# Whole 128x128 transposes with one wide copy each, and GpSimd for the normalization, in a gated linear attention + spatial gating kernel

## The chip, the cores and the metric

The kernel runs on one core of a Trainium2 chip, in one launch. The metric is the device time in microseconds (us); lower is better. The time before is 144.26 us, the median of three runs (143.81 to 145.1).

## What is computed

Two layers follow each other. The first is a gated linear recurrence over 768 steps for 4 batches and 8 heads of width 48; its output is laid out as x (768 rows of 384 per batch). The second is a gated MLP whose second half is normalized per row and mixed along the sequence.

```python
for t in range(S):
    state = alpha[:, :, t, :, None] * state + np.einsum('bhd,bhe->bhde', k[:, :, t], v[:, :, t])
    y[:, :, t] = np.einsum('bhd,bhde->bhe', q[:, :, t], state)
...
h = np.maximum(x @ w_in, 0.0)
u, v = (h[..., :d_ff // 2].copy(), h[..., d_ff // 2:].copy())
v_n = (v - mu) / np.sqrt(var + 1e-06)
v_s = np.einsum('ts,bsd->btd', w_spatial, v_n) + b_spatial[None, :, None]
gated = u * v_s
return (gated @ w_out).astype(np.float32)
```

## The kernel before

**The recurrence in chunks.** Each batch has 6 chunks of 128 steps, 24 in all. Within a chunk the recurrence is done by matmuls: cumulative sums of log(alpha) (`cum`, TensorE), their exponentials (`einv`, `eexp`, ScalarE), the scaled k and q (`kt`, `qt`), the transposes of both (`tr`), scores k·q (`sc`), a causal mask on VectorE (`m`, `ms`), the product with v plus the part that comes from the old state (`y`), and a copy of the result as xT (`xe`). The state goes from chunk to chunk by `upd` (TensorE), `z` (VectorE, an add out of PSUM), `S` (multiply by the decay) and `sb` (a bf16 copy).

**Three layouts of chunks.** Chunks 0 and 1 are a *pair* (`pair`, j = 0): two chunks are loaded together, two steps to a partition, so that 64 partitions hold a chunk. Chunks 2 to 5 and 6 to 9 are two *groups of four* (`four_chunks`, j = 1 and 3), 32 partitions to a chunk. All others are loaded one by one (`single`, called from `two_singles`). In the pair and in the groups of four, k and q are turned by transposes of 64 rows: for each half of the partitions (`r`) one transpose per head pair, 16 for each of k and q and each half group, into two PSUM banks, and each bank is copied by its own instruction of 128x512 (`ev`, lines 564 to 568 and 780 to 789).

**The MLP.** Per batch and chunk: `v` (x times the second half of w_in, 3 matmuls of 512 columns), `ve` (relu into v_sb), `bn` (statistics, VectorE), `rs` (1/sqrt(var), two ScalarE steps for two chunks at a time), `vn` (subtract and multiply: the normalized rows, line 1103), and `u` for the other half, transposed. `s` mixes along the sequence with w_spT as the moving operand: part 0 takes the first four chunks of vn, part 1 the last two. `se` adds the bias, `g` multiplies with u, `o` is the product with w_out, `oe` its copy and `st` the store.

**What sets the order.** All operations are listed once with their dependencies, and the text `PLAN` is then read word by word: a letter for the engine (P TensorE, D VectorE, A ScalarE, G GpSimd, S the DMA queue), the operation's number, and for TensorE the PSUM banks. Every engine does its words in this order. Parts such as `:512#2` are matmuls on a tile `junk` (line 247) that feed nothing. Each w_* weight is loaded into one of two buffers `raw_w` (fetch, line 1052), cast to bf16 on some engine, and the buffer's next load waits for these casts: w_in (two halves), w_spatial (three pieces, turned into w_spT by `wt` and `we`), w_out.

Of the kernel before, what the change touches and what calls it, by code (L numbers as in the profile page):

```python
# [16 lines left out]
BF16 = mybir.dt.bfloat16  # L17
# [30 lines left out]
D154 S16 A143 A14 G13 D165 S274 P162@5,2 G155 D166 G17 G18 S20 A169 P54@3 A55 P96@0 A163 D157 A97 P183@2,1 A19
P170@4,3 S23 S276 D184 D185 D172 G158 D160 P99@5 A100 P167@2 A168 P177@0,6 P175@1,5 A182 A176 D171 D179 P188@2 P193@7
A189 A194 D178 D190 D101 D98 P197@1 A198 G159 G156 P173@6 A174 G161 P186@7 A187 P180@1 P199@6 A181 P222@1 D223 G278  # L50
A281 A200 D201 A102 P206@7 A207 D208 G279 P218@0 P209@1 G21 P34@7,6 A219 S389 S275 A202 D203 A210 G280 G10 G22 P191@0
P216@2 A282 D36 D35 A192 P37@1,6 A38 D211 A212 D103 D105 D104 D39 D213 G24 P40@7,4 A42 A217 P286@5 D41 D204 D205
P220@0 D221 P292@1 A287 D215 A293 G25 P43@3,6 D45 D44 D214 A294 D306 P283@7 P289@4 A284 A285 A288 A290 P236@2 P195@0
G305 G299 P232@6 P237 A291 G397 D297 P228@3 S26 P229 P233 D300 D303 G27 A28 A295 A196 D238 G296 G302 P317@4,5 P46@1,7
A318 P49@2,0 D230 D48 D234 G231 D47 G235 A319 A51 S387 S277 P224@3 S29 P225 D226 G227 A50 G301 P314@1,5 P311@0,6 D315
D312 P308@2,4 D310 A304 P248@3 P249 A309 D250 P340@4,2 D342 D341 A316 A30 P334@5,0 A313 D335 D336 P244@1 S493 P245
P240@6 S386 A390 A298 G32 S398 A31 G239 A497 P241 P391@5 A392 S388 S399 A393 A402 D242 D246 G307 P320@4,2,3,7 D321
G322 G395 D33 A394 D323 S400 S496 S505 S401 D324 G325 P332@6,0 A339 A333 P252@1 P253 P403@4 A404 D254 D326 D396 G406
A405 P262@2 A263 D407 P259@0 A260 P343@1 P337@3 A338 D344 P345@5,2 S495 S547 A346 S559 A352 P353@0,6 D354 D355 G327
G255 G328 G251 S550 S506 P409@4,3 A411 A410 D329 P347@5,1 D349 D348 P412@2 P358@0 P256@6 A257 P361@7 A359 P420@4,1  # L60
P415@5,6 G330 D331 D413 A509 P350@0 A351 P356@2 A357 D421 P498@4 S494 A362 A501 P368@0 P373@2 A369 P371@7 A551 D416
D422 G243 G247 D417 G408 G414 S549 P423@0 P418@6 D504 S507 A424 A499 A500 P510@1 A511 P265@0 D363 A372 S560 A513 A266
D419 D503 A512 P379@6 P441@5 A380 P425@7 A426 P428@0 P268@6 P435@7 D360 D370 S508 A364 S548 S622 S561 S613 A442 A429
D381 A382 D365 D366 D367 P377@4 P375@5 D515 S717 A436 A269 S623 S610 S611 S562 G514 G502 D427 D430 A376 A378 A431 D383
D384 P520@0 P437@1 A438 S625 P517@7,3 A563 D385 D432 P439@5 P552@4 P271@6 D519 D521 D433 A553 P447@1 P564@0 P451@3
D434 P448 P452 A554 A374 D557 A565 G568 A566 A272 S783 P455@2 P456 P443@6 G522 G621 A555 A518 P523@7,4 A440 S612 D556
D453 D569 A626 A567 P532@5,3 D457 D449 D525 D524 D533 D534 G516 S720 S624 P571@2,1 A573 A572 G454 G458 P444 P627@4
P528@0 D529 D445 S729 G558 A614 P467@7 P468 P526@5 A527 G450 G446 P535@3 D469 A536 A721 A628 G630 P578@0,2 D580 G470
D579 S771 S846 P587@1,6 P615@5 D530 A616 P574@7 P540@3 A541 P722@2 P537@0 A617 P475@3 D575 D588 A538 A570 S261 P463@7
A632 A618 S718 S719 G576 P583@1 D589 A531 D584 P481@0 P459@6 D620 G619 P636@5 P471@1 P472 A787 P464 P460 A482 A723  # L70
D539 D542 D473 A577 A629 A476 P581@0 P590@1 D631 S834 S732 S730 A725 P633@4,3 G585 A586 S731 D637 D465 G638 G466 A582
A733 P592@0 A591 P603@1 P734@7 D634 D728 D461 D462 A635 P644@6,3 P639@4,5 D645 A593 A737 A604 A543 A735 P599@0 A600
A724 D640 G474 G738 P487@1 P490@6 P597@0 A491 D641 P642@5 A736 D646 P647@3 A643 D594 D727 D544 D605 A488 A648 P484@6
A775 P649@1 D650 D651 D546 P652@3 S773 A653 A485 D654 D545 A606 D607 D608 D609 P595@2 A596 P663@1 P776@3 A779 S784
P665@6 A666 P478@5 P659@2 G726 G740 P601@6 D739 D602 A777 A660 P788@4 P679@2 P661@7 P744@6 A479 A778 D781 A655 S772
S785 D656 D664 D745 A789 A790 A791 G792 D658 D662 P667@5 P741@1,3 P675@6 D793 S835 A657 P676 P752@4 P668 D677 G780
# [24 lines left out]
SMALL = ()  # L101
# [1170 lines left out]
```

## Time and profile before

| | |
|---|---|
| median of three runs | 144.26 us (143.81 to 145.1) |
| the profiled execution | 145.11 us |
| its span in the trace | 142.5 us |
| TensorE busy | 133.9 us (94%) |
| VectorE busy | 121.6 us (85%) |
| ScalarE busy | 108.6 us (76%) |
| GpSimd busy | 83.6 us (59%) |
| `junk` matmuls (line 247) | 11.7 us in the page's groups |

The profile is of one execution. The span runs from the first to the last recorded instruction; the profiled execution lasted 2.6 us longer than its span. PE is TensorE, PEld its weight loads, DVE VectorE, ACT ScalarE, POOL GpSimd, SP the engine whose queue issues the DMAs. Matmuls are pipelined, so that a row's duration for a group includes about 0.17 us in which the next group already runs; the distance from one start to the next is the cost. L1010 is a helper (`accumulate`) for all of `v`, `u`, `s` and `o`, L192 one for all products, L181 and L183 for all copies of ScalarE and of the two others: such groups are told apart by their tiles.

### The profile page before, as it was taken

How to read it: one execution, taken by the hardware profiler on the slowest of the kernel's cores; microseconds unless marked ns; L12 is line 12 of the kernel's file. 1: busy time of each engine (PE TensorE's matmuls, PEld its weight loads, DVE VectorE, ACT ScalarE, POOL GpSimd, SP SyncE). 2: the span in 40 equal slices, each digit the busy share in tenths (PEclk: the TensorE clock that was granted, in tenths of full speed). 3: DMA queues.
4: the chain of work that ended last, by engine and by line, in shares of the span. 5: the costliest groups of instructions: out<-in, count | busy, mean ns of one | idle time of the engine just before them, and what ended most of it. 6: DMA issues, size and time to landing. Idle time of an engine off the chain costs nothing.

```text
span 142.5 us, 5286 instructions
## 1 busy us (share of the span) xinstructions
PE 133.9 (94%) x2124; PEld 80.9 (57%) x2136; DVE 121.6 (85%) x281; ACT 108.6 (76%) x253; POOL 83.6 (59%) x138
## 2 busy tenths in 40 slices
PE   7999979999989999799999998999999999999990
PEld 3546545565656656565667556656665765555560
DVE  6398697999997999989989999989979999877820
ACT  3465867999979889689998998879978666853261
POOL 7363695799489589813077956700599665000970
PEclk9999999999999999999999999999999999999999
DMA  4999992899999898989999998979930341027044
GB/s 114 335 365 362 391 391 66 265 373 294 301 238 291 165 207 170 192 167 178 201 211 205 187 208 161 229 211 247 187 60 5 110 162 66 5 94 292 0 164 167
DMA packets 76520, 28.64 MB, mean 201 GB/s; under 512 B 63057, under 2 KB 74961, under 8 KB 76497
## 3 DMA queue, kind: packets, MB, share of 16 engines
q1 hardware_dynamic: 76464, 28.32, 75.9%
q8 instruction: 16, 0.26, 0.7%
q14 instruction: 8, 0.06, 0.1%
q0 software_dynamic: 32, 0.00, 0.0%
HBM read 23.60 MB, written 4.72 MB: 199 GB/s over the span
## 4 chain that ended last, share of the span: by engine, by line
PE 67%; DVE 12%; DMA 8%; issue 4%; POOL 4%; ACT 3%; ACTq 0%; DVEq 0%; POOLq 0%; SPq 0%
PE bank L1010 44%; DMA raw_w<-in_moe_w_spatial_dram 8%; PE bank L247 5%; DVE qt L192 2%; PE bank L965 2%; PE bank L993 2%; DVE ptm L954 2%; POOL ac L192 2%; PE bank L948 2%; PE bank L438 1%; DVE zs L415 1%; PE bank L723 1%; PE bank L936 1%; PE bank L905 1%; PE bank L800 1%
## 5 line engine op out<-in xcount | busy, mean ns | idle before, releaser
L1010 PE MATMUL bank<-w_spT,vn 128*128 128x384 bf16 x192 | 35.3, 326 | 0.1
L192 POOL TENSOR_TENSOR kt<-kc,binv 128x384 bf16<-128x384 f32 x22 | 20.2, 932 | 25.9 <-ACT binv L912 19.0
L192 POOL TENSOR_TENSOR gT<-vs,uT 128x384 bf16<-128x384 f32 x28 | 26.6, 969 | 14.6 <-DVE vs L1159 14.6
L1010 PEld LDWEIGHTS <-vn 128*128 128x128 bf16 x192 | 17.7, 97 | 11.6 <-issue 0.6
L181 ACT COPY kqT<-bank 128x1024 bf16<-128x1024 bf16 (+1 forms) x23 | 17.9, 812 | 4.7 <-PE bank L777 1.9
L1159 DVE TENSOR_TENSOR vs<-bank,bsp_bc 128x384 f32<-128x384 f32 x31 | 16.4, 549 | 3.8 <-PE bank L1010 2.7
L1010 PE MATMUL bank<-xT,w_in 128*128 128x384 bf16 x96 | 19.4, 326 | 0.0
L1010 PE MATMUL bank<-w_out_sb,gT 128*128 128x384 bf16 (+1 forms) x100 | 18.4, 319 | 0.0
L954 DVE TENSOR_TENSOR ptm<-bank,mask 128x512 bf16<-128x512 f32 x28 | 17.6, 678 | 0.1
L1010 PE MATMUL bank<-w_in,xT 128*128 128x512 bf16 x60 | 16.7, 379 | 1.0 <-issue 0.2
L1072 DVE BATCH_NORM_STATS2 stats<-v_sb 128x6 f32<-128x512 bf16 x24 | 16.3, 680 | 0.6 <-ACT v_sb L187 0.5
L187 ACT ACTIVATE uT<-bank 128x384 bf16<-128x384 f32 x25 | 12.1, 489 | 4.8 <-PE bank L1010 4.8
L187 ACT ACTIVATE v_sb<-bank 128x512 bf16<-128x512 f32 x22 | 13.1, 602 | 1.7 <-PE bank L1010 1.4
L192 DVE TENSOR_TENSOR qt<-qc,bank 128x384 bf16<-128x384 f32 x24 | 12.4, 542 | 2.3 <-ACT bank L514 1.8
L181 ACT CAST xT<-bank 128x384 bf16<-128x384 f32 x20 | 9.2, 482 | 4.7 <-PE bank L438 3.9
L1010 PEld LDWEIGHTS <-gT 128*128 128x128 bf16 x100 | 9.3, 97 | 6.2
L247 PE MATMUL bank<-junk 128*128 128x512 f32 (+5 forms) x22 | 11.7, 653 | 1.0 <-DVE quarters_of L324 1.0
L1010 PEld LDWEIGHTS <-w_in 128*128 128x128 bf16 x96 | 8.8, 98 | 6.5
L850 DVE TENSOR_TENSOR ptm<-bank,mask 128x512 bf16<-128x512 f32 x16 | 10.1, 679 | 0.3 <-PE bank L842 0.2
L1010 PEld LDWEIGHTS <-xT 128*128 128x128 bf16 x72 | 6.4, 97 | 6.1 <-ACT xT L181 0.6
L415 DVE TENSOR_TENSOR zs<-bank,state 128x384 f32<-128x384 f32 x16 | 8.7, 545 | 0.1
L1103 DVE TENSOR_SCALAR vn<-v_sb,mvs,rstd 128x512 bf16<-128x512 bf16 x21 | 8.1, 419 | 0.2 <-ACT rstd L1083 0.2
(165 smaller groups left out, 260.6 us busy)
## 6 DMA issues: line engine op xcount, KB each, us to landing
vc<-in_v_dram SPq DMA_DIRECT2D x14, 192.0 KB, 3.9
kc<-in_k_dram SPq DMA_DIRECT2D x14, 192.0 KB, 4.2
ac<-in_alpha_dram SPq DMA_DIRECT2D x14, 192.0 KB, 4.3
qc<-in_q_dram SPq DMA_DIRECT2D x14, 192.0 KB, 4.6
raw_w<-in_moe_w_spatial_dram SPq DMA_DIRECT2D x3, 768.0 KB, 4.9
out_dram<-raw_w SPq DMA_DIRECT2D x11, 192.0 KB, 2.1
out_dram<-o_sb SPq DMA_DIRECT2D x9, 192.0 KB, 2.0
ac<-in_alpha_dram SPq DMA_DIRECT2D x2, 768.0 KB, 8.0
```

Of the source, the lines that this page charges most:

```text
L181: nc.scalar.copy(out=out, in_=in_)
L187: nc.scalar.activation(out=out, in_=in_, func=AF.Relu)
L192: ENG[eng].tensor_tensor(out=out, in0=in0, in1=in1, op=ALU.mult)
L247: nc.tensor.matmul(out=banks[n][:, 0:cols].rearrange("p (a b) -> p a b", a=4), lhsT=junk, rhs=junk[:, None, 0:cols // 4].to_broadcast([128 ...
L415: lambda _: nc.vector.tensor_tensor(out=zs[i % 3], in0=tp(), in1=state[(i - 1) % 3], op=ALU.add),
L850: nc.vector.tensor_tensor(out=ptm[n2][:, ci, s], in0=banks[sl.bank].rearrange("p (hp t) -> p hp t", hp=HP), in1=mask[:, 3][:, None, :].to_ ...
L948: nc.tensor.matmul(out=pt[s][:, hp, :], lhsT=kT[rows, hp, :], rhs=qT[rows, hp, :], start=True, stop=True)
L954: nc.vector.tensor_tensor(out=ptm[n2][:, ci, s], in0=banks[sl_p[s].bank].rearrange("p (hp t) -> p hp t", hp=HP), in1=mask[:, 2][:, None, : ...
L1010: nc.tensor.matmul(out=ps, lhsT=lhsT, rhs=rhs, start=first and n == 0, stop=last and n == len(pairs) - 1)
L1072: nc.vector.bn_stats(out=stats[tt % 2], in_=v_sb[n2][:, tt, :])
L1103: nc.vector.tensor_scalar(out=vn[n2][:, x, :], in0=v_sb[n2][:, x, :], scalar1=mvs[n2][:, x, 0:1], scalar2=rstd[n2][:, x:x + 1], op0=ALU.su ...
L1159: nc.vector.tensor_tensor(out=vs[d], in0=banks[sl.bank][:, 0:TH], in1=bsp_bc[:, th, :], op=ALU.add)
```

## The change

**Transposes.** In `pair` and `four_chunks` the 16 transposes of 64 rows become 8 of 128 rows by 128 columns, into one PSUM bank, and the two copies of 128x512 become one of 128x1024 (`evs`). Ten such sets are concerned (k and q of j = 0, and of the two halves of j = 1 and j = 3): 80 fewer transposes, 20 narrow copies less, 10 wide ones more. So that one copy can fill what were two tiles, `kqT[0]` and `kqT[1]` are now two views of one tile `kq`.

**Normalization.** `vn` may run on GpSimd, by the same instruction as on VectorE.

**The order table** is new throughout. VectorE did 21 of the 24 `vn` and does 5; ScalarE did 3 and does 1; GpSimd does 18. The `junk` columns go from 4512 to 3248. Some 70 other operations change engine, mostly in both directions; on balance GpSimd gets two more state copies and four more casts of v. PAIRS, QUADS and the dependencies of the other operations stand as they were. Lines below the first edit are up to five lower than before.

```diff
 PLAN = """
-D4 G9 D0 D3 G6 D2 S56 A60 G11 G5 P61@0:512#0:512#0:288#0 A63 A64 P62@1 A65 D1 D8 A67 A66 S58 D69 S57 S106 G71 D68
...
+D2 G6 G11 D0 S56 A60 G9 G5 P61@0:512#0:512#0:288#0 D4 D3 A63 D1 G7 D8 P62@1 A65 A66 P54@2:232#2 S57 D68 S58 D72 S59
...
-    kqT = sb("kqT", 2, [128, 2, 2, HP * 128])
+    kq = consts.tile([128, 2, 2, 2, HP * 128], BF16, name="kq")
+    kqT = [kq[:, :, 1 - x] for x in range(2)]
...
-            sls = [Slot(), Slot()]
-
-            def tr(_, src=(kt, qt)[n], sls=sls):
-                to = [half_words(sl, 8, 64) for sl in sls]
+            sl_w = Slot()
+
+            def tr(_, src=(kt, qt)[n], sl=sl_w):
+                to = half_words(sl, 16, 64).rearrange("p (r x) t -> p r x t", r=2)
                 for par in range(2):
                     for hp in range(HP):
-                        for r in range(2):
-                            rows = half(r)
...
-                                nc.tensor.transpose(
-                                    to[r][:, HP * par + hp, :], src[rows, par, hp].rearrange("p s d -> p (s d)"),
-                                    ident[rows, rows])
...
+                        nc.tensor.transpose(
+                            to[:, :, HP * par + hp, :], src[:, par, hp].rearrange("p s d -> p (s d)"), ident)
...
+            o = op(("evs", nm, j), "DVE ACT",
+                   lambda e, n=n, sl=sl_w: copy(
+                       e, kqT[n2][:, n].rearrange("p r x -> p (r x)"), banks[sl.bank].bitcast(BF16)),
+                   [("tr", nm, j)] + old_turned, use=[sl_w])
             for r in range(2):
-                op(("ev", nm, j, r), "DVE ACT",
-                   lambda e, n=n, r=r, sl=sls[r]: copy(e, kqT[n2][:, n, r], banks[sl.bank].bitcast(BF16)[:, 0:512]),
-                   [("tr", nm, j)] + old_turned, use=[sls[r]])
+                made[("ev", nm, j, r)] = o
...
+                def ev(e, n=n, x=x, sl=sl_w):
+                    to = kq[:, n].rearrange("p z ci (hp t) -> p (z ci) hp t", hp=HP)[:, :, :, 64 * x:64 * x + 64]
+                    copy(e, to, banks[sl.bank].bitcast(BF16).rearrange("p (zc hp t) -> p zc hp t", zc=4, hp=HP))
...
-                nc.vector.tensor_scalar(
+                ENG[e].tensor_scalar(
                     out=vn[n2][:, x, :], in0=v_sb[n2][:, x, :], scalar1=mvs[n2][:, x, 0:1],
                     scalar2=rstd[n2][:, x:x + 1], op0=ALU.subtract, op1=ALU.mult)
 
-            op(("vn", b, x), "DVE ACT", vnf,
+            op(("vn", b, x), "DVE ACT POOL", vnf,
```

**Where the order moves: VectorE in the pair.** The first rows are those of before, from the pair's first product with q; `ptm` are the masked scores, `state_128<-bank` is `S` of chunk 0, `zs` is `z` of chunk 1, and the last rows are the products with q of the first group of four.

```order
L192 TENSOR_TENSOR qt_106<-qc,bank_64 128x8x48
L192 TENSOR_TENSOR kt_104<-kc,binv_108 128x8x48
L192 TENSOR_TENSOR qt_106<-qc,bank_65 128x8x48
L183 COPY kqT_112<-bank_64 128x512
L183 COPY kqT_112<-bank_67 128x512
L183 COPY kqT_112<-bank_65 128x512
L602 TENSOR_TENSOR ptm_117<-bank_65,mask 128x512
L602 TENSOR_TENSOR ptm_117<-bank_64,mask 128x512
L602 TENSOR_TENSOR ptm_117<-bank_67,mask 128x512
L183 CAST bsp_bc<-bank_69 128x384
L602 TENSOR_TENSOR ptm_117<-bank_66,mask 128x512
L192 TENSOR_TENSOR state_128<-bank_66,bc_119 128x384
```

And the same place of the change:

```order
L191 TENSOR_TENSOR kt_104<-kc,binv_108 128x8x48
L191 TENSOR_TENSOR qt_106<-qc,bank_65 128x8x48
L191 TENSOR_TENSOR qt_106<-qc,bank_64 128x8x48
L182 COPY kq<-bank_67 128x1024
L191 TENSOR_TENSOR state_127<-bank_65,bc_118 128x384
L415 TENSOR_TENSOR zs_125<-bank_68,state_127 128x384
L595 TENSOR_TENSOR ptm_116<-bank_69,mask 128x512
L595 TENSOR_TENSOR ptm_116<-bank_67,mask 128x512
L595 TENSOR_TENSOR ptm_116<-bank_64,mask 128x512
L595 TENSOR_TENSOR ptm_116<-bank_66,mask 128x512
L191 TENSOR_TENSOR qt_106<-qc,bank_70 128x8x48
L191 TENSOR_TENSOR qt_106<-qc,bank_68 128x8x48
```

Three narrow copies have become one wide one, the state of chunk 0 and the sum for chunk 1 stand ahead of the masked scores instead of behind them, and the bias copy (`bsp_bc`) has gone to ScalarE.

**ScalarE ahead of the first w_in cast.** Before, from the last exponential of the first group of four to the casts that free the weight buffers:

```order
L749 ACTIVATE bank_67<-bank_67 128x384
L181 CAST xT_134<-bank_66 128x384
L181 COPY kqT_113<-bank_70 128x4x2x64
L181 CAST o_sb_158<-vc 128x384
L181 COPY kqT_112<-bank_65 128x4x2x64
L181 COPY kqT_112<-bank_69 128x4x2x64
L181 COPY kqT_113<-bank_68 128x4x2x64
L181 COPY kqT_112<-bank_64 128x4x2x64
L181 CAST w_in_88<-raw_w_96 128x512
```

Of the change:

```order
L744 ACTIVATE bank_64<-bank_64 128x384
L180 CAST bsp_bc<-bank_67 128x384
L180 COPY kq<-bank_71 128x16x64
L180 CAST o_sb_157<-vc 128x384
L180 COPY kq<-bank_68 128x16x64
L180 CAST xT_133<-bank_69 128x384
L180 CAST xT_133<-bank_66 128x384
L180 CAST w_in_88<-raw_w_96 128x512
```

Five narrow copies ahead of the cast have become two wide ones; a bias copy and a second xT copy have come in.

**GpSimd ahead of the first mix.** Before, from the last of the products of alpha for the second group of four; `w_row` are casts of w_spatial:

```order
L192 TENSOR_TENSOR ac<-ac 128x8x48
L355 MEMSET le_one 128x128
L356 AFFINE_SELECT le_one<-le_one 128x128
L355 MEMSET mask 128x128
L356 AFFINE_SELECT mask<-mask 128x128
L183 CAST w_row_94<-raw_w_96 128x768
L183 CAST w_row_95<-raw_w_97 128x768
L183 CAST w_row_93<-raw_w_97 128x768
L192 TENSOR_TENSOR kt_104<-kc,binv_109 128x8x48
L192 TENSOR_TENSOR kt_105<-kc,binv_111 128x8x48
L183 CAST vb_116<-vc 128x8x48
L183 CAST w_row_94<-raw_w_96 128x768
```

Of the change:

```order
L191 TENSOR_TENSOR ac<-ac 128x8x48
L182 CAST w_row_93<-raw_w_97 128x768
L182 CAST w_row_95<-raw_w_97 128x768
L1098 TENSOR_SCALAR vn_141<-v_sb_139,mvs_145,rstd_147 128x512 x4
L191 TENSOR_TENSOR kt_104<-kc,binv_109 128x8x48
L191 TENSOR_TENSOR kt_104<-kc,binv_108 128x8x48
L191 TENSOR_TENSOR kt_105<-kc,binv_110 128x8x48
L182 CAST w_row_94<-raw_w_96 128x768
```

Four `vn` stand between the casts of w_spatial and the products with k of the second group of four; the four instructions that make `le_one` and a mask stand earlier now, ahead of the casts of w_in.

More of the change, by code (lines that the diff above doesn't have):

```diff
@@ L48 @@
[L48 to L52, printed above, removed]
@@ L669, in four_chunks @@
     def four_chunks(j):
+        assert j % 2
         b, c0 = divmod(2 * j, NCH)
```

120 lines of the change are left out of this document (57 added, 63 removed).

## The prediction

> **What bounds the kernel now.** I read the page's totals first, then the windows, then the chain that ended last.
>
> ```profile
> PE 133.9 (94%) x2124; PEld 80.9 (57%) x2136; DVE 121.6 (85%) x281; ACT 108.6 (76%) x253; POOL 83.6 (59%) x138
> ```
>
> ```profile
> 60.00:70.00 10.00, 9.95 (x148) 6.00 (x148) 9.22 (x23) 9.27 (x28) 1.89 (x3) 1.00 0.92 181
> ...
> 120.00:130.00 10.00, 9.95 (x110) 6.00 (x111) 7.76 (x20) 7.22 (x18) 0.00 (x0) 1.00 0.28 103
> ```
>
> The first number of a window is its sum, then come PE, PEld, DVE, ACT, POOL, the granted clock and the DMA share. From 60 on TensorE has no gaps, and VectorE is close behind it; GpSimd has holes of 8 and 10 us in these two windows. So behind the start the time is TensorE's work, and it falls only if TensorE gets less work or starts earlier. What holds it at the start stands in the chain:
>
> ```profile
> 7.78 1.31 DVE kt L192
> 9.09 0.47 DVE qt L192
> ...
> 9.61 0.41 PE bank L550 x16
> 10.02 1.03 PE bank L247 x2
> 11.05 0.57 PE bank L593 x32
> ...
> 15.09 0.49 PE bank L575 x16
> 15.58 0.56 DVE state L192
> ...
> 17.23 1.93 DVE qt L192 x4
> 19.16 1.36 DVE o_sb L183 x2
> ...
> 22.30 0.43 DVE kqT L183
> ...
> 22.75 0.63 ACT w_in L181
> ...
> 23.43 4.19 DMA raw_w<-in_moe_w_spatial_dram
> ```
>
> The pair and the first group of four run as one chain over VectorE and TensorE, with `junk` matmuls in the gaps. ScalarE's narrow copies of the group stand ahead of its w_in cast, this cast frees the buffer, and only then does the load of w_spatial go out. That the buffer and not the memory was late, the queue's own waits say (us in all, times, longest):
>
> ```profile
> SPq L1052 <- ACT w_in L181: 11.5, 2, 9.4
> ```
>
> **The change part by part.**
>
> *Transposes.* The timeline of TensorE around three sets of before:
>
> ```profile
> 42.38 1.15 PE L1010 MATMUL bank<-w_spT,vn 128*128 128x384 bf16 x6
> 43.46 0.41 PE L777 MATMUL bank<-ident,kt 64*128 64x64 bf16 x16
> 43.70 0.40 PE L777 MATMUL bank<-ident,qt 64*128 64x64 bf16 x16
> 43.93 0.40 PE L777 MATMUL bank<-ident,kt 64*128 64x64 bf16 x16
> 44.26 1.15 PE L1010 MATMUL bank<-w_spT,vn 128*128 128x384 bf16 x6
> ...
> 54.55 0.33 PE L936 MATMUL bank<-vb,kt 128*128 128x96 bf16 x4
> 54.76 0.81 PE L1010 MATMUL bank<-w_in,xT 128*128 128x512 bf16 x2
> ```
>
> A set of 16 costs 0.24 us from start to start: the two halves run side by side, 64 columns in 30 ns. Six matmuls of 384 columns take 1.15 - 0.17 = 0.98, which is 0.42 ns a column, so about 0.1 us lies between L1010 and L777, and as much behind the last set. Eight whole transposes have 1024 columns one after the other: 0.43 us at that rate from below; from above by the L936 row, 0.21 / 4 = 52 ns for 96 columns, 70 ns for 128, 0.56 a set. I take 0.45. In batch 0's mix four sets in two groups cost 4 x 0.24 + 2 x 0.2 = 1.36 us and will cost 1.8 (to 2.24): **+0.45 us** (to +0.9), on the path. The six sets of the start fall into stretches filled with `junk`, where I count them in the chain below.
>
> *Copies.*
>
> ```profile
> L181 ACT COPY kqT<-bank 128x1024 bf16<-128x1024 bf16 x12 | 11.9, 1014 | 1.4 <-PE bank L993 1.4
> L181 ACT COPY kqT<-bank 128x512 bf16<-128x512 bf16 x11 | 6.0, 592 | 3.3 <-PE bank L777 1.9 <-PE bank L550 1.4
> L1103 DVE TENSOR_SCALAR vn<-v_sb,mvs,rstd 128x512 bf16<-128x512 bf16 x21 | 8.1, 419 | 0.2 <-ACT rstd L1083 0.2
> L183 DVE COPY kqT<-bank 128x512 bf16<-128x512 bf16 x9 | 3.5, 416 | 0.7 <-PE bank L777 0.7
> L183 DVE COPY kqT<-bank 128x1024 bf16<-128x1024 bf16 x2 | 1.4, 688 | 0.1
> ```
>
> ScalarE had 11 x 0.592 = 6.5 us and gets 5 x 1.014 = 5.1; VectorE had 9 x 0.416 = 3.7 and gets 5 x 0.688 = 3.4. That is 1.7 us off two engines that aren't the bound; it counts where the copies stand in the chain. VectorE also loses 16 `vn`, 16 x 0.419 = 6.7 us.
>
> *The start, by its own rows.* The pair's scores come no earlier: kt (1.31, as GpSimd makes the other one beside it), two qt (0.54 each), two sets and a wide ScalarE copy of 1.01 put them at 11.0, as before. But `upd` now stands ahead of the scores, so the state and the sum for chunk 1 (0.56 each) are done before the four masked products (0.68 each), which end near 14.9. Then VectorE has four qt (0.54), one kt (1.0, between 0.55 alone and the 1.31), one cast of v (0.72) and two wide copies (0.69): 14.9 + 2.2 + 1.0 + 0.7 + 1.4 is about 20.3, with little idle, where before its last kqT copy ended at 22.73. ScalarE ends its last exponential near 16.6 instead of 17.66, as the cumulative sum that it waits for no longer stands behind `upd` on TensorE, then has the bias copy 0.49, kq 1.01, a cast 0.52, kq 1.01 (behind a set that ends at 18.1), two xT copies 0.96 and the w_in cast 0.63, together 4.6: 21.3 with the hops, against 23.38. **The load of w_spatial goes out 2.1 us earlier**, and the first projection likewise. Nine additions of rows with two or three waits guessed: I give it 1.0 to 3.0.
>
> What if the data is late instead?
>
> ```profile
> raw_w<-in_moe_w_in_dram SPq DMA_DIRECT2D x2, 768.0 KB, 8.7
> ```
>
> ```profile
> L1052 SPq DMA_DIRECT2D raw_w<-in_moe_w_in_dram x2: 1067/1104/1140, 11.0 to 12.2; - x2
> ```
>
> The loads of w_in were issued at 11.0 and 12.2 and land a median 8.7 us later, 19.7 and 20.9. So the casts may begin at 19.7, just when GpSimd and ScalarE get there; the loads hide none of the 2.1, but more than that is not to be had.
>
> *GpSimd takes 18 `vn`.* No row shows this operation there.
>
> ```profile
> L192 POOL TENSOR_TENSOR gT<-vs,uT 128x384 bf16<-128x384 f32 x28 | 26.6, 969 | 14.6 <-DVE vs L1159 14.6
> L183 POOL CAST w_in<-raw_w 128x512 bf16<-128x512 f32 x4 | 2.5, 642 | 0.0
> L332 POOL TENSOR_SCALAR_AFFINE_SELECT lt_pair<-lt_pair 128x128 bf16<-128x128 bf16 x1 | 0.3, 292 | 0.0
> ```
>
> From below 0.64 us, a cast of the same 512 columns; from above 969 x 512 / 384 = 1.29, a product of two tensors. The select has one tensor and more than one step: 0.29 for 128 columns, and with 0.1 of start (a memset of one column takes 0.10) 0.87 for 512. I take T = 0.85, 15 us in all, most of it in the holes. Does TensorE wait for it? At each batch the slack is what TensorE still has to do:
>
> - Batch 0: before, the first mix began at 37.34, with one `u` still behind it. Now 37.34 - 2.1 + 0.5 for that `u` is 35.7. GpSimd's casts of w_spatial, which ended at 35.64, end near 31.7: the 2.1, one less cast ahead of them (0.82) and the 1.0 us of `le_one` and its mask moved forward. Four T later is 35.1. Slack 0.6; at 1.29 a stall of 1.2.
> - Batch 1: after `v` of chunk 3 TensorE has 5.3 us until the mix (L1010 groups by columns, one `upd`, one `trk`); relu 0.60, statistics 0.68 + 0.18, ScalarE 0.50, a matmul's tail and hops take 2.3, then up to three T: 4.85. At 1.29 a stall of 0.9, and 0.2 at the next part.
> - Batch 2 keeps three `vn` on VectorE. Batch 3: 4.4 us of TensorE against 2.3 + 2T = 4.0; at 1.29 a stall of 0.5.
>
> ```profile
> 33.28 2.36 POOL L183 CAST w_row<-raw_w 128x768 bf16<-128x768 f32 x3
> 37.70 2.05 POOL L192 TENSOR_TENSOR kt<-kc,binv 128x384 bf16<-128x384 f32 x2 [2.07 <-ACT binv L746]
> ```
>
> ```profile
> 37.34 0.81 PE L1010 MATMUL bank<-w_spT,vn 128*128 128x384 bf16 x4
> ```
>
> Behind the four `vn` on GpSimd wait the products with k for the second group of four; they had 2.07 us of slack there. So **0** for this part, +2.8 at the upper bound.
>
> [...]
>
> *VectorE relieved.* TensorE's waits on VectorE past the start:
>
> ```profile
> PE bank L861 <- DVE zs L415: 0.7, 1, 0.7
> PE bank L800 <- DVE kqT L183: 0.5, 1, 0.5
> PE bank L948 <- DVE vs L1159: 0.5, 1, 0.5
> ```
>
> They are 1.7 us; with 9 us less on VectorE some of it goes. I take **-0.3** (0 to -1.5). The end stays: last store, same width.
>
> **The sum.** -2.1 + 0.45 + 0 - 0.3 is about -2.0. The profiled execution took 145.11 us, of which 142.5 is the span: I expect about 143.1 for one like it. It lies 0.85 above the median of 144.26, so for the median **142.3 us**. About 1%, 1.4 us, is what a measurement of this kernel can tell from no change.
>
> **The rivals.**
>
> *The start's gain is given back.* The order behind the start is new everywhere, and TensorE was full; a place where two engines now meet badly costs 0.5 to 1 us (as L861 did), and two or three of them plus transposes at 0.56 a set (+0.9) eat the 2.1. For it: VectorE at 9 tenths in the windows, all places new. Against it: VectorE has 8% less to do, and so has the place where before waited. The time is 144.3, between 143.6 and 145.
>
> *GpSimd becomes the link before each mix.* If its `vn` takes 1.6 us, the stalls are 31.7 + 6.4 - 35.7 = 2.4 in batch 0, 2.3 + 4.8 - 5.3 = 1.8 and 0.4 in batch 1, 2.3 + 3.2 - 4.4 = 1.1 in batch 3: 5.7, on top of 142.3: 148.0. For it: two engines on SBUF at once do slow each other here: VectorE's kt took 1.31 us beside GpSimd's, and `vn` itself spreads far:
>
> ```profile
> L1103 DVE TENSOR_SCALAR vn<-v_sb,mvs,rstd x21: 380/405/694, 35.1 to 129.1; 128x512 bf16<-128x512 bf16 x21
> ```
>
> Against it: GpSimd's own rows are steady (0.91 to 0.93 for nearly all kt). It decides from T = 1.25, where the stalls equal the gain, and makes the kernel slower by over 1% from T of about 1.4. [...]
>
> **How the numbers follow.** Forecast 0.55, gain given back 0.27, GpSimd the link 0.18. Within the forecast nine in ten are more than 1.4 us faster; given back, a quarter are, and an eighth are slower by that much; with GpSimd the link, five in six are slower. Faster 0.58, within 1% 0.24, slower 0.18. For the range: down, -3.0 + 0.3 - 1.0 and some more is -4.2, 140.0; up, the second case and the near part of the third, to 146.0.
>
> **What would show it.** Right: the first load of w_spatial goes out near 21.3; sets of 8 transposes start 0.45 us apart; `vn` on GpSimd 0.65 to 1.0; the first mix starts near 35.7 and TensorE's windows from 40 on are as full as before. The prediction is wrong if TensorE waits for `vn` by more than 1 us in all, if that load goes out after 22.5, or if the first mix is early and the end is not.

## The result and the profile after

The change makes the kernel slower: 161.85 us median (160.65 to 162.43, 4 runs) against 144.68 for the kernel before on the same chip (143.81 to 146.2, 4 runs), a ratio of 1.120 [1.110, 1.130]. The profiled execution took 161.98, of which 160.2 is the span. Ratios, with 95% intervals in square brackets, leave out executions more than 1.5% slower than the fastest of the same kernel; medians and ranges hold all of them. (Lines of the file are some 5 lower than before: L1005 is the projections and the mix, L1098 `vn`, L771 the transposes of a group.)

First the totals of the page and the row of the granted clock, then GpSimd's costliest group:

```profile
PE 139.0 (87%) x2042; PEld 83.9 (52%) x2054; DVE 114.7 (72%) x256; ACT 104.4 (65%) x242; POOL 122.7 (77%) x162
...
PEclk9999999999699999999579999999999999956999
```

```profile
L1098 POOL TENSOR_SCALAR vn<-v_sb,mvs,rstd 128x512 bf16<-128x512 bf16 x18 | 37.5, 2097 | 8.0 <-ACT rstd L1078 8.0
```

TensorE went from 94% to 87% of a longer span, and three dents appear in its clock. GpSimd is busy 39 us more, 37.5 of them in the 18 `vn`: one takes **2.1 us** where the prediction put 0.85 and at most 1.29. TensorE's own waits name it:

```profile
PE bank L1005 <- POOL vn L1098: 13.5, 5, 4.8
PE bank L1005 <- DVE kt L191: 1.1, 1, 1.1
```

How one such wait comes about is seen in the timelines of GpSimd and of TensorE around the first mix:

```profile
32.70 8.43 POOL L1098 TENSOR_SCALAR vn<-v_sb,mvs,rstd 128x512 bf16<-128x512 bf16 x4
41.10 2.65 POOL L191 TENSOR_TENSOR kt<-kc,binv 128x384 bf16<-128x384 f32 x3
```

```profile
36.03 0.33 PE L1005 MATMUL bank<-w_spT,vn 128*128 128x384 bf16 x1
41.18 4.62 PE L1005 MATMUL bank<-w_spT,vn 128*128 128x384 bf16 x17 [4.83 <-POOL vn L1098]
```

TensorE is at the mix at 36.03 (before: 37.34), multiplies with the one tile that is there, and waits 4.83 us for the last of four; this is the wait in brackets. Then 17 matmuls of 384 columns take until 45.63, where the transposes begin: 0.26 us each, where the prediction's row of six gave 0.163. The windows (sum; PE, PEld, DVE, ACT, POOL; granted clock; DMA) tell why:

```profile
40.00:42.00 2.00, 0.82 (x4) 0.42 (x5) 0.00 (x0) 0.00 (x0) 2.00 (x3) 0.85 1.01 309
42.00:44.00 2.00, 2.00 (x8) 0.99 (x7) 0.00 (x0) 0.00 (x0) 2.00 (x4) 0.50 1.08 266
44.00:46.00 2.00, 2.00 (x16) 1.19 (x15) 0.72 (x2) 0.00 (x0) 1.39 (x2) 0.80 0.88 175
46.00:48.00 2.00, 2.00 (x42) 1.37 (x40) 1.32 (x4) 1.44 (x3) 1.53 (x3) 1.00 1.08 208
```

Windows of 0.2 us put the granted clock at 0.50 from 41.4 to 44.8, and at that clock eight matmuls fill a window of 2 us. In batch 1 it is at 0.50 from 75.5 to 82.3, so it falls within the wait of 4.44, and in batch 3 from 140.4 to 147.2. VectorE and ScalarE stand still meanwhile (their 0.00 in the first two windows): they wait for the mix.

```profile
77.65 2.42 PE L1005 MATMUL bank<-w_spT,vn 128*128 128x384 bf16 x7 [4.44 <-POOL vn L1098]
...
137.62 0.50 PE L1005 MATMUL bank<-w_spT,vn 128*128 128x384 bf16 x2 [0.97 <-POOL vn L1098]
139.68 0.34 PE L1005 MATMUL bank<-w_spT,vn 128*128 128x384 bf16 x1 [1.56 <-POOL vn L1098]
141.74 6.26 PE L1005 MATMUL bank<-w_spT,vn 128*128 128x384 bf16 x21 [1.72 <-POOL vn L1098]
```

TensorE works 3.4, 4.7 and 5.5 us at the clock of 0.50 in the three places; half of these 13.6, 6.8 us, is what the slow clock takes.

Two terms of the prediction can be read off as well: the load of w_spatial goes out at 22.36 (before 23.43), and a set of eight whole transposes costs 0.45 us from start to start:

```profile
45.63 0.61 PE L771 MATMUL bank<-ident,kt 128*128 128x128 bf16 x8
46.08 1.14 PE L1005 MATMUL bank<-w_spT,vn 128*128 128x384 bf16 x6
```

### The profile page after: what moved, and what is told of

Its sections match the earlier page's. It is cut to its first block, busy times and chain, and to the rows that moved or that the text cites. A ratio compares the mean times of both kernels' runs of the same rounds, so it can differ in the third digit from the quotient of the medians.

```text
span 160.2 us, 5122 instructions
## 1 busy us (share of the span) xinstructions
PE 139.0 (87%) x2042; PEld 83.9 (52%) x2054; DVE 114.7 (72%) x256; ACT 104.4 (65%) x242; POOL 122.7 (77%) x162
## 4 chain that ended last, share of the span: by engine, by line
PE 61%; POOL 11%; ACT 7%; issue 7%; DMA 6%; SPq 3%; DVE 2%; DVEq 0%; POOLq 0%; ACTq 0%
PE bank L1005 43%; POOL vn L1098 11%; DMA qc<-in_q_dram 6%; PE bank L943 2%; PE bank L960 2%; SPq L463 2%; PE bank L771 2%; PE bank L438 2%; PE bank L988 2%; SPq L681 1%; PE bank L900 1%; PE bank L931 1%; ACT uT L186 1%; PE bank L837 1%; PE bank L247 1%
## 5 line engine op out<-in xcount | busy, mean ns | idle before, releaser
L1005 PE MATMUL bank<-w_spT,vn 128*128 128x384 bf16 x192 | 42.1, 367 | 14.7 <-POOL vn L1098 13.5
L1098 POOL TENSOR_SCALAR vn<-v_sb,mvs,rstd 128x512 bf16<-128x512 bf16 x18 | 37.5, 2097 | 8.0 <-ACT rstd L1078 8.0
L1005 PEld LDWEIGHTS <-vn 128*128 128x128 bf16 x192 | 19.6, 108 | 31.2 <-POOL vn L1098 16.9
L191 POOL TENSOR_TENSOR gT<-vs,uT 128x384 bf16<-128x384 f32 x29 | 26.7, 930 | 8.8 <-DVE vs L1154 8.5
L180 ACT COPY kq<-bank 128x1024 bf16<-128x1024 bf16 x15 | 15.1, 1013 | 14.8 <-PE bank L771 7.9
L191 POOL TENSOR_TENSOR kt<-kc,binv 128x384 bf16<-128x384 f32 x21 | 19.3, 936 | 7.0 <-ACT binv L907 4.5
L1005 PE MATMUL bank<-xT,w_in 128*128 128x384 bf16 x96 | 19.4, 332 | 0.0
L1005 PE MATMUL bank<-w_out_sb,gT 128*128 128x384 bf16 (+1 forms) x100 | 18.0, 319 | 0.0
L1005 PE MATMUL bank<-w_in,xT 128*128 128x512 bf16 x60 | 16.9, 380 | 1.0 <-issue 0.5
L186 ACT ACTIVATE uT<-bank 128x384 bf16<-128x384 f32 x24 | 11.4, 492 | 6.9 <-PE bank L1005 6.9
L180 ACT COPY raw_w<-bank 128x384 f32<-128x384 f32 (+1 forms) x11 | 5.1, 469 | 14.7 <-PE bank L1005 14.7
L1005 PEld LDWEIGHTS <-w_in 128*128 128x128 bf16 x96 | 9.1, 99 | 7.0 <-issue 0.5
L1005 PEld LDWEIGHTS <-gT 128*128 128x128 bf16 x100 | 9.4, 97 | 6.4 <-issue 0.4
L247 PE MATMUL bank<-junk 128*128 128x512 f32 (+5 forms) x20 | 9.4, 596 | 1.4 <-DVE junk L1233 1.1
L180 ACT CAST xT<-bank 128x384 bf16<-128x384 f32 x21 | 9.8, 491 | 1.0 <-PE bank L438 0.9
```

The lines of the kernel that those rows point to most:

```text
L180: nc.scalar.copy(out=out, in_=in_)
L186: nc.scalar.activation(out=out, in_=in_, func=AF.Relu)
L191: ENG[eng].tensor_tensor(out=out, in0=in0, in1=in1, op=ALU.mult)
L247: nc.tensor.matmul(out=banks[n][:, 0:cols].rearrange("p (a b) -> p a b", a=4), lhsT=junk, rhs=junk[:, None, 0:cols // 4].to_broadcast([128 ...
L1005: nc.tensor.matmul(out=ps, lhsT=lhsT, rhs=rhs, start=first and n == 0, stop=last and n == len(pairs) - 1)
L1098: ENG[e].tensor_scalar(out=vn[n2][:, x, :], in0=v_sb[n2][:, x, :], scalar1=mvs[n2][:, x, 0:1], scalar2=rstd[n2][:, x:x + 1], op0=ALU.subtr ...
```

## The experiments

Medians are device us; "before" is the kernel before on the same chip as the version at hand. Four chips were used, with medians of before from 144.44 to 144.96.

### What the operation costs by itself

Nine forms of GpSimd's instruction, four of each, behind the work of the kernel before; the first of them:

```diff
+    ts = nc.gpsimd.tensor_scalar
+    mu, rs_ = mvs[0][:, 0, 0:1], rstd[0][:, 0:1]
+    si, so = v_sb[0], vn[0]
...
+    for r in range(4):
+        ts(out=so[:, r, :], in0=si[:, r, :], scalar1=mu, scalar2=rs_, op0=ALU.subtract, op1=ALU.mult)
...
```

> The kernel before with nine forms of GpSimd instruction, four of each, appended behind all work; the time is longer by them and tells nothing. It tells what makes vn 2.08 us. If the two pointers to per-row scalars do it, the same with two constants falls to 0.7 or less; if the two steps do it, the form with one step and a pointer falls to about half and the one with two constants stays near 2; if bf16 does it, the one from float32 to float32 falls and the plain bf16 copy is above 0.64.

Eight of the groups by form, the second number behind the bar being the mean in ns:

```profile
L1245 POOL TENSOR_SCALAR vn<-v_sb,mvs,rstd 128x512 bf16<-128x512 bf16 x4 | 8.3, 2070 | 0.0
L1247 POOL TENSOR_SCALAR vn<-v_sb,mvs,rstd 128x128 bf16<-128x128 bf16 x4 | 3.1, 792 | 0.0
L1249 POOL TENSOR_SCALAR vn<-v_sb,rstd 128x512 bf16<-128x512 bf16 x4 | 6.2, 1566 | 0.0
L1251 POOL TENSOR_SCALAR vn<-v_sb 128x512 bf16<-128x512 bf16 x4 | 7.6, 1935 | 0.0
L1253 POOL TENSOR_SCALAR vn<-v_sb 128x512 bf16<-128x512 bf16 x4 | 5.9, 1506 | 0.0
L1255 POOL COPY vn<-v_sb 128x512 bf16<-128x512 bf16 x4 | 2.3, 633 | 0.0
L1259 POOL TENSOR_SCALAR vn<-raw_w,mvs,rstd 128x512 bf16<-128x512 f32 x4 | 8.3, 2084 | 0.0
L1261 POOL TENSOR_TENSOR vn<-v_sb 128x512 bf16<-128x512 bf16 x4 | 4.5, 1169 | 0.0
```

The 2.07 us are the operation's own: the first group begins at 135.45, while the last results are still copied out, but nothing runs beside its last two instructions, and its four range only from 2.066 to 2.080. Float32 input (2.08) makes no difference, constants in place of the per-row columns little (1.94), one step instead of two 0.43 to 0.50. What is dear is the tensor-scalar form: one step of it (1.51 to 1.57) costs more than a product of two tensors (1.17) and over twice a copy (0.63). So the prediction's upper bound, a two-tensor product, was no bound for this form.

### The same order with a short `vn`

Two runs leave the order of the changed kernel as it is and shorten GpSimd's `vn`; both leave the normalization out there. The first:

```diff
+if e == "POOL":
+    nc.gpsimd.tensor_copy(out=vn[n2][:, x, :], in_=v_sb[n2][:, x, :])
+    return
 ENG[e].tensor_scalar(
```

> The changed kernel with its order untouched; GpSimd's 18 vn are plain copies of v (128 x 512 bf16), so the output lacks the normalization there. The appended copy of this shape took 0.633 us against 2.07 for the tensor-scalar with two steps. Theory 'duration' (the order and the sum were right, only T was mis-sized): with T = 0.64 inside the bounds of the prediction TensorE waits for vn by under 1 us in all, the first mix runs through from about 36.0, no window past 40 has a granted clock under 0.9, and the time is 142.3 plus what the transposes cost beyond +0.45 (their run alone gave +2.1 us, so +1.7): 142.5 to 144.5. Rival 'the order lost it' (VectorE's version of the same order still took 146.4 with 4.8 us of waits for vn, so other work is late there): 146 or more, with waits of TensorE on something else than vn.

Measured 138.82 (138.31 to 139.06), ratio 0.961 [0.956, 0.966], below both expectations. But this copy no longer waits for the statistics. In the second run GpSimd copies one column of rstd ahead of each (`+nc.gpsimd.tensor_copy(out=seen[n2][:, x:x + 1], in_=rstd[n2][:, x:x + 1])`), and so waits for them:

> As the run with plain copies, but GpSimd first copies one column of rstd, so that each of its vn still waits for the statistics as the real one does (the plain copy waited for v alone); the normalization is left out. T is then about 0.64 + 0.1, near the 0.85 of the prediction. Theory 'only T was mis-sized': 138.5 to 141, TensorE's waits for vn under 1.5 us in all. Rival 'the plain copies were fast because they no longer waited for the statistics': 142 or more, with TensorE waiting for vn or what stands before it.

Measured **139.15** (138.62 to 140.21), ratio 0.962 [0.953, 0.970]. The one wait that TensorE's timeline shows past the start, its first mix, and the window of all that lies behind it:

```profile
59.72 0.41 PE L961 MATMUL bank<-ptm,vb 128*32 128x128 bf16 x16 [1.21 <-DVE ptm L950]
```

```profile
35.30 3.09 PE L1006 MATMUL bank<-w_spT,vn 128*128 128x384 bf16 x18
```

```profile
35.30:138.40 103.10, 98.32 (x1505) 61.59 (x1503) 87.75 (x173) 76.21 (x182) 70.80 (x122) 1.00 0.72 172
```

There is no wait for `vn`, 18 matmuls run in one go, and the mean clock behind the first mix is 1.00. With a copy of 0.62 us, inside the prediction's bounds for T, the order does what was forecast and 3 us more, and the time lies where 'only T was mis-sized' has it.

### How the time grows with T

```diff
+if e == "POOL":
+    nc.gpsimd.tensor_scalar(out=vn[n2][:, x, :], in0=v_sb[n2][:, x, :], scalar1=rstd[n2][:, x:x + 1],
+                            scalar2=None, op0=ALU.mult)
+    return
```

> The changed kernel, order untouched; GpSimd's 18 vn multiply by rstd only (one step, the mean is not subtracted), which took 1.57 us in the run of the forms. Theory 'waits in proportion to T plus a slow clock behind each long one': from T = 2.08 to 1.57 the waits of batch 0 lose 4 x 0.5, of batch 1 3 x 0.5, of batch 3 2 x 0.5, so 13.5 falls to about 9, and the clock loss of about 4 us to some 3: 154 to 157. The prediction's rival formula at T = 1.6 gave stalls of 5.7 and 148.0: it holds if the time is 147 to 150 and the clock stays at 0.95 or more past 40.

Measured 150.55 (148.45 to 152.38), ratio 1.034 [1.024, 1.043], with T = 1.56 by its row. The first expectation is not met. Two of the four executions, 148.45 (the profiled one) and 150.0, lie in the range of the second, but its condition on the clock holds only for the mean (0.985): in one place it falls to 0.50. TensorE's waits, the first mix and that of batch 1:

```profile
PE bank L1005 <- POOL vn L1099: 7.0, 4, 2.6
```

```profile
38.01 2.94 PE L1005 MATMUL bank<-w_spT,vn 128*128 128x384 bf16 x17 [2.61 <-POOL vn L1099]
```

```profile
70.55 2.32 PE L1005 MATMUL bank<-w_spT,vn 128*128 128x384 bf16 x7 [2.19 <-POOL vn L1099]
```

The waits are 7.0 where the prediction's rival formula gives 5.7 for T = 1.6. Of three places only batch 1 has the slow clock. The 2.61 us of batch 0 left it at full speed (17 matmuls in 2.94), the 2.19 us of batch 1 did not (seven in 2.32). So the loss isn't in proportion to the wait, and no length of wait divides the two cases.

What divides them is where the wait lies. In the changed kernel the clock changes at 41.4, 44.8, 75.5, 82.3, 140.4 and 147.2, and the distances are 1, 9, 2, 17 and 2 times 3.41 us; in this version it falls at 70.7 and is back at 74.1, again 3.41 later. So in these executions it changes only at marks that are 3.41 us apart. Counted back from 70.7, a mark at 36.6 cuts the wait of batch 0 into 1.2 and 1.4 us, while the whole 2.19 of batch 1 lies between two marks. The stretches between marks fit this: in the changed kernel, in this version and in one below (all of the normalization on VectorE) every stretch at full clock in which TensorE idled 2.18 us or more was followed by one at 0.50, and none with 1.71 or less was. (In the two versions with narrow copies in the new order it also fell at the start, after stretches with some 1.2 to 1.6 us idle that hold many small transposes; no run shows why less sufficed there.)

### The slow clock by itself

Matmuls on constants are put into the waits; the waits themselves stay. In batch 0, batch 1 and batch 3:

```diff
+FILL = {(0, 2, 0): {1: [(4, 512)] * 5}, (1, 2, 0): {1: [(6, 512)] * 5},
+        (3, 1, 0): {0: [(2, 512)], 2: [(2, 512), (2, 256)], 3: [(2, 512)] * 2}}
...
+for n, cols_ in FILL[b, d, th].get(st, ()):
+    warm(cols_, n, "#")
```

> The changed kernel with junk matmuls (float32, 512 columns) set into TensorE's waits for GpSimd's vn: five in batch 0 ahead of the second product of the first mix, five at the same place of batch 1, and one, one and a half and two in batch 3. Theory 'a long wait costs twice, once itself and once by the slow clock behind it': the waits of 13.5 us are still there as time (filled now), but the matmuls behind them run at full clock. Between the changed kernel and the one with plain copies TensorE's busy time differs by 139.0 - 131.9 = 7.1 us at equal work, and this goes: 154 to 157.5, and the 17 matmuls of the first mix take near 2.9 us instead of 4.62. Rival 'the clock is not lowered by the wait': within 1.5 us of the changed kernel (160 to 163.5).

Measured 157.38 (156.11 to 158.37), ratio 1.086 [1.076, 1.096]: 4.5 us below the changed kernel, as the first expectation has it.

```profile
35.21 4.56 PE L247 MATMUL bank<-junk 128*128 128x512 f32 x10 [0.25 <-DVE uT L188]
39.80 0.66 PE L1141 MATMUL bank<-w_spT,vn 128*128 128x384 bf16 x3
40.29 2.44 PE L1005 MATMUL bank<-w_spT,vn 128*128 128x384 bf16 x14
```

The same 17 matmuls go through in 2.9 us instead of 4.6, and the granted clock is 1.00 until the last matmuls are done. The wait is paid as a wait, and again as a slow clock. Not all of the 4.5 us is the clock: in the profiled execution the four `vn` begin at 31.31 and in that of the changed kernel at 32.70, so that 1.4 of the 4.4 us between the two spans come from an earlier start and 3.0 from what lies behind it.

### The old order, and the parts by themselves

The normalization of these 18 tiles on GpSimd in the order of before (18 words of `PLAN` change their letter from D to G), with nothing else changed:

```diff
-nc.vector.tensor_scalar(
+ENG[e].tensor_scalar(
     out=vn[n2][:, x, :], in0=v_sb[n2][:, x, :], scalar1=mvs[n2][:, x, 0:1],
```

> The kernel before with the same 18 vn on GpSimd, at the places that VectorE had them in its order; nothing else changed. If GpSimd's vn is the cause, the old kernel loses as much by it: 157 to 163 us, vn rows of 2.07 us and a clock that drops behind the waits. If the new order is the cause, it stays below 150.

Measured 169.91 (169.37 to 170.03), ratio 1.177 [1.172, 1.181], above the 157 to 163 of the first expectation. So the loss does not come from the new order: the old one loses 25 us, the new 17. In the old order TensorE waits not only for `vn` but for the casts and the product that stand behind it on GpSimd:

```profile
PE bank L1009 <- POOL vn L1102: 7.5, 2, 5.8
PE bank L1021 <- POOL w_row L182: 6.4, 2, 4.1
PE bank L935 <- POOL kt L191: 4.4, 1, 4.4
```

The old order with the cheap `vn` that waits for the statistics (the normalization left out on GpSimd; the edit is that of the run with 139.15):

> The kernel before (its order, its half-row transposes), with the same 18 vn as cheap copies on GpSimd behind the copy of one column of rstd; the normalization is left out there. Tells what a short vn on GpSimd gives without the new order and the whole transposes. Theory 'the gain is the new order's (the start and the places)': 143 to 145, as VectorE's waits in the old order were 1.7 us in all and its GpSimd is at 59%. Rival 'any order gains once VectorE is relieved': 139 to 141.5.

Measured 147.19 (146.78 to 147.61), ratio 1.017 [1.008, 1.026]: 2 to 3 us slower than before, and neither expectation.

```profile
35.34 0.35 PE L1022 MATMUL bank<-ident,w_row 64*128 64x64 bf16 x12 [1.39 <-POOL w_row L182]
...
69.74 0.34 PE L936 MATMUL bank<-vb,kt 128*128 128x96 bf16 x4 [1.62 <-ACT rstd L1083]
```

Even a `vn` of 0.6 us on GpSimd pushes its casts of w_spatial (`w_row`) and its products behind waits for statistics there. Relief of VectorE alone does not make the old order faster. The price of the dear `vn` against the short one is the same in both orders: 169.91 - 147.19 = 22.7 here and 161.85 - 139.15 = 22.7 in the new one.

The transposes and wide copies alone, in the old order, each set's wide copy at the place of its first narrow one:

```diff
-P74@0,2:512#2:512#2:112#2 D72 P77@1,3 D75 S107 D79 A76 D78
+P74@0:512#2:512#2:112#2 D72 P76@1 A75 S105 D77
```

> The kernel before with the whole transposes and the wide copies alone, in the old order (each wide copy at the place of the first of its two narrow ones, five on ScalarE and five on VectorE). By the prediction's terms: +0.45 us of TensorE in batch 0's mix, the start near the same: 144 to 145.5 us. A rival by which the transposes cost a part of the loss gives over 147; one by which they bring the gain of the start by themselves gives below 143.

Measured 146.58 (146.51 to 146.59), ratio 1.016 [1.012, 1.019], between the expectation of 144 to 145.5 and the rival's 147.

```profile
24.00 0.40 PE L836 MATMUL bank<-kq 48*128 48x128 bf16 x8 [0.32 <-DVE kq L181]
...
38.30 0.81 PE L1004 MATMUL bank<-w_spT,vn 128*128 128x384 bf16 x4
...
40.03 2.46 PE L1004 MATMUL bank<-w_spT,vn 128*128 128x384 bf16 x14 [0.43 <-DVE w_spT L181]
```

The first mix is at 38.30 instead of 37.34, 0.96 later, and from there to the end of the span it takes 106.00 us instead of 105.16, another 0.84. The 0.84 is what four sets of the mix give at 0.45 instead of 0.24, 4 x 0.21; the gaps around them, 0.2 us a group, which the prediction let go with the old sets, are still there. The 0.96 arises between 21 and 24 us, where sets are longer too and TensorE waits 0.42 for a cast and 0.32 for the wide copy that the scores need. By the medians it is +2.1 us where the prediction had +0.45. The opposite test puts the half-row transposes and two narrow copies into the new order:

```diff
-P76@0:512#3:240#3 G71 P74@3 D75 G73 A70 A67 P78@1,4 A55 A77
+P77@0,5:512#3:240#3 G71 P74@3,4 D75 D76 G73 A70 A67 P80@1,4 A55 A78 A79
```

> The new order with cheap vn on GpSimd that wait for the statistics (139.15 us in its run), but with the half-row transposes and two narrow copies a set of the kernel before, both on the engine that made the wide one; each set takes a second bank that stands free. The normalization is left out on GpSimd. Theory 'whole transposes cost +2.1 us in any order' (their run alone in the old order): 136.5 to 138. Theory 'the new order hides them; the 2.1 were places of the old order': 138.5 to 140.5. Theory 'the wide copy pays' (one of 0.69 or 1.01 us stands for two of 0.42 or 0.59, and a set waits for one engine less): 141 or more, with TensorE waiting for kqT at the start.

Measured 144.51 (143.09 to 145.25) against 139.15: 5.4 us slower, the third expectation.

```profile
20.06 0.64 PE L777 MATMUL bank<-ident,qt 64*128 64x64 bf16 x32 [0.91 <-DVE kqT L182]
21.61 0.86 PE L800 MATMUL bank<-o_sb,kt 32*128 32x96 bf16 x48 [0.91 <-ACT kqT L180]
...
46.08 1.14 PE L1010 MATMUL bank<-w_spT,vn 128*128 128x384 bf16 x6 [0.91 <-DVE kqT L182]
```

The waits are for the copies, at the start above all; the first mix moves from 35.30 to 38.64. Part of this is the clock, which is at 0.50 from 23.3 to 26.7, at most 1.7 us; but two of the ten executions had a granted clock of 0.998 and 1.0, and took 143.09 and 144.05. A set of whole transposes costs TensorE more (0.45 us against 0.24), as predicted. That what it buys is a set out of PSUM by one copy fits the waits, but the order was made for whole sets, and what another order with half-row ones would give is not shown.

### Versions with the whole computation

All 18 `vn` back on VectorE, at the places that GpSimd had (`-G102 +D102`, and so on):

> The changed kernel with its 18 GpSimd vn given back to VectorE at the same places of the order; all else as changed. If the loss is GpSimd's vn alone (2.08 us each instead of the 0.85 taken, TensorE idle behind it and then on a slow clock), this runs as forecast for a cheap vn: 142 to 143.5 us, first mix near 36, granted clock 1.00 throughout. If the new order or the whole transposes carry part of the loss, it stays above 146.

Measured 146.44 (146.22 to 148.19), ratio 1.017 [1.011, 1.024], the second expectation's time; but TensorE waits for `vn` 4.8 us in four places, as VectorE comes to them late, and behind the 2.18 us of one of them the clock is at 0.50 from 71.6 to 75.1. Then these are moved up, right behind their statistics:

```diff
-G102 A201 D205 A287 ... D202 A206 D197 G198 D217 G199 P280@7 G103
+D102 D197 D103 D198 D199 A201 D205 A287 ... D202 A206 D217 P280@7
```

> The changed kernel with all vn of the 18 on VectorE, and moved up in the order to stand right behind the statistics' nm of their pair of tiles. Theory 'duration': the 4.8 us of waits for vn that the version with GpSimd's places had go down to under 1.5, the first mix starts near 35.6 and runs through, time 142 to 144.5. Rival 'VectorE has no room': what vn no longer loses, the products, relus and w_spT copies pushed back behind it lose, time 145.5 to 147.

Measured 145.73 (145.61 to 146.22), ratio 1.010 [1.007, 1.013], the rival's time. The wait for `vn` is down to 0.2, and this took its place:

```profile
PE bank L959 <- DVE ptm L948: 1.2, 1, 1.2
PE bank L1004 <- DVE qt L190: 1.1, 1, 1.1
...
PE bank L899 <- DVE qt L190: 1.0, 1, 1.0
PE bank L1004 <- DVE w_spT L181: 0.9, 1, 0.9
```

The same with the half-row transposes, whose two narrow copies were put on VectorE and on ScalarE:

> The new order with vn on VectorE early as in the run before, but with the old half-row transposes and two narrow copies a set (one on VectorE, one on ScalarE); the second bank of each set is one that stands free. Theory 'transposes cost +2.1 us wherever they stand' (+2.1 in the old order alone): 2.1 us less than the run with whole transposes, and the first mix about 1 us earlier. Rival 'the new order was made for whole transposes and hides them': within 0.7 us of the run with whole ones. If both hold what the first theory says, this one is at 140 to 142 and below both kernels.

Measured 153.92 (151.75 to 155.24); even the fastest execution is 6 us slower than with whole ones. Both expectations fail. It points the same way as the run above, but since the narrow copies also changed engines, and the clock is at 0.50 twice in the start (11.2 to 14.6 and 24.9 to 28.3), it doesn't price the one copy.

Next, six `vn` of 2.07 us stay on GpSimd, where the short `vn` had shown over 2 us of slack, and eighteen are VectorE's:

```diff
-G102 A201 D205 A287 A289 A288 P40@4,6 D41 ... D42 D300 D202 A206 D197 G198 D217 G199 P280@7 G103
+G102 D197 D103 D198 D199 A201 A287 A289 A288 P40@4,6 D41 ... D42 D205 D300 D202 A206 D217 P280@7
```

> The changed kernel with the full computation: GpSimd keeps only six vn of 2.07 us (one of batch 0, two of batch 1, two of batch 2, one of batch 3), those whose statistics are ready over 2 us ahead of the mix in the run with plain copies; the other eighteen are VectorE's and stand right behind their statistics, the statistics of the fifth tile of batch 0 behind the w_spT copy that was waited for. Theory 'the order is good for 139 once no vn is late': the 5 us of waits that VectorE's version had (w_spT 0.9, ptm 1.2, qt 1.0 and 1.1, v 0.6) fall to 1 to 3: 140 to 143, below the kernel before. Rival 'VectorE has no room for them': 144.5 to 146.5 as with all on VectorE.

Measured **141.96** (141.74 to 145.47), ratio 0.980 [0.971, 0.988]: below both kernels, with the full result, as the first expectation has it. Three of its four executions lie at 141.74 to 142.03, so the gain of 2% rests on few. Past the start three waits are left:

```profile
35.64 0.32 PE L708 MATMUL bank<-la,lt_quad 128*128 128x384 bf16 x1 [0.46 <-DVE qt L190]
69.26 1.46 PE L1004 MATMUL bank<-w_spT,vn 128*128 128x384 bf16 x8 [0.79 <-DVE qt L190]
97.75 0.82 PE L1004 MATMUL bank<-w_spT,vn 128*128 128x384 bf16 x4 [0.49 <-DVE vn L1097]
```

One more move of VectorE's `vn` and statistics by these three waits (words of the order alone):

> As the run with vn spread by slack (141.96 us, full computation), with VectorE's vn and statistics moved once more by the waits that were left (qt 0.8 and 0.5, vn 0.5): the third and fourth tile of batch 0 behind the product with q that TensorE waited for, those of batches 1 and 2 behind the statistics of the next tile, and the last pair's statistics earlier on ScalarE. Theory 'those 1.8 us are places': 140 to 141.5. Rival 'VectorE has no more room, a move only shifts the wait': 141.5 to 143.

Measured 144.43 (143.52 to 145.83), ratio 0.999 [0.996, 1.003]. That is above both expectations, over twelve executions. In the profiled one, which was the slowest (145.83), waits of 0.9 to 1.5 us came up at other places (for `qt`, `kq`, `ptm`, `uT`). This move shifted waits and removed none of the time; whether another would is not shown.

## Why the prediction was wrong, point by point

- **The step that failed** is the bound of the unknown cost: "from below 0.64 us, a cast of the same 512 columns; from above 969 x 512 / 384 = 1.29, a product of two tensors". It measured 2.07. The rows used were of other forms, and an upper bound from an operation with more inputs is no bound where the form itself is dearer. The select row that decided for 0.85 was no better a relative: with two steps on 128 columns the tensor-scalar takes 0.79 where that row had 0.29. So the term "**0** for this part, +2.8 at the upper bound" became waits of 13.5 us.
- **The mechanism stood there, as a rival.** "GpSimd becomes the link before each mix" names the place, and its formula for T = 2.08 gives 31.7 + 8.3 - 35.7 = 4.3 in batch 0 (measured 4.83), 2.3 + 6.24 - 5.3 = 3.2 in batch 1 (4.44) and 2.3 + 4.16 - 4.4 = 2.1 in batch 3 (0.97 + 1.56 + 1.72 = 4.25: four tiles stand one behind the other on GpSimd from 133.43 on, where the formula counted two). It priced the case at 148.0 and gave it 0.18; the range ended at 146.
- **What no term held: the slow clock.** From the short `vn` that waits for the statistics to the changed kernel the span grows by 160.2 - 138.4 = 21.8. TensorE's idle time has 21.2 - 7.0 = 14.2 of it, and its busy time for the same matmuls 139.0 - 131.4 = 7.6, near the 6.8 that the three places at 0.50 give. The run with filled waits got some 3.0 of it back as time. The traces show the 0.50, the marks 3.41 us apart and the 3.4 or 6.8 us until the clock is back; why it falls no run shows, nor why 2.19 us sufficed in one place and 2.61 did not in another, beyond where the marks cut the two waits.
- **Right: the start.** The load of w_spatial at 22.36 in the changed kernel, 21.4 and 21.6 in the runs with a short `vn` (predicted 21.3), the first mix reached at 36.0 and 35.3 (predicted 35.7). In this execution VectorE's first product with q of the group waits 1.14 us for q's data and starts at 15.83, against 14.24 and 15.11 in those two; the sum had no wait for q.
- **Right in its row, wrong in its meaning: the transposes.** A set costs 0.45, as the sum had it. But behind the first mix of the old order the four sets cost 0.84 and not 0.45, and outside the start's chain the copies had no term: alone in the old order the pair of edits costs 2.1, and taking it out of the new order costs 5.4, of which at most 1.7 is the slow clock.
- **Too small: what the order gains behind the first mix.** There the span had 105.16 us before, with 99.07 of TensorE's work; with the short `vn` that waits for the statistics 103.10 with 98.32. That is 2.1 less, of which 0.5 is the `u` that now stands ahead of the mix; so 1.6 less where the sum had +0.45 - 0.3, and 1.3 of it are gaps. With the 0.4 by which the first mix is earlier than predicted the span is 138.4 against the sum's 140.5. Another 0.8 of the 3 us between 142.3 and 139.15 lies outside the span: the profiled execution lasts 1.8 us longer than its span, that of before 2.6, and no run shows why. The "9 us less on VectorE" did not come from the prediction's rows, which give 6.7 + 0.3 = 7.0; in the changed kernel it is 121.6 - 114.7 = 6.9.

Open is what each move of the new order gives by itself: the runs with the parts alone stood in orders that weren't made for them. The price of a part is shown for that order only.

## What to carry to other kernels

An operation that no row shows on the engine it moves to has no upper bound from its cousins: measure it alone behind the kernel, or take the range up to the point where its slack is gone several times over. To see whether an order is good apart from such a cost, keep the order and put the cheapest operation with the same waits in its place; here that told 139 from 162, and where in the order six of the dear ones could stay. A long wait on TensorE is to be priced with the matmuls behind it at half clock as well: in the three versions compared above every stretch at full clock between two marks with 2.18 us or more idle was followed by one at 0.50, and in the changed kernel 3.4 to 5.5 us of TensorE's work ran so at each place.

## What the runs showed of the hardware that was not expected

- GpSimd's tensor-scalar on 128 x 512 bf16 takes 1.51 to 1.57 us with one step and 1.94 to 2.07 with two, (2070 - 792) / 384 = 3.3 ns a column with two, against 1.17 for a product of two tensors and 0.63 for a copy; VectorE does the two steps in 0.41.
- TensorE's granted clock went to 0.50 in or just behind waits of 4.83, 4.44 and 2.19 us and three in a row of 0.97, 1.56 and 1.72, stayed at full behind one of 2.61, and came back after 3.4 or 6.8 us. In the changed kernel and with the one-step `vn` it changed only at marks 3.41 us apart, and 2.18 us of idle time between two marks sufficed with all `vn` on VectorE.
- Beside work on the other engine VectorE's `vn` spreads far, GpSimd's little: in the version with six on GpSimd these take 2076 to 2236 ns, VectorE's eighteen 383 to 998. But three of VectorE's, of 0.40 us each (32.73 to 33.78), ran inside one of GpSimd's (32.01 to 34.25): there the two engines' `vn` ran at once. The one of 998 ns, at 96.7, ran beside GpSimd's products with k (94.84 to 97.55).

```profile
L1097 DVE TENSOR_SCALAR vn<-v_sb,mvs,rstd x18: 383/407/998, 32.7 to 125.3; 128x512 bf16<-128x512 bf16 x18
L1097 POOL TENSOR_SCALAR vn<-v_sb,mvs,rstd x6: 2076/2084/2236, 32.0 to 120.5; 128x512 bf16<-128x512 bf16 x6
```
